# A gated mix of sliding-window attention and an MLP: the row maxima get a rate of their own by stage

## The chip, the cores and the metric

The kernel runs on one core of a Trainium2 chip. What counts is the device time of one execution, in microseconds. Engines go by the names of the profile: PE is the TensorE matmul engine (PEld its weight loads), DVE VectorE, ACT ScalarE, POOL GpSimd, SP the SyncE engine, which issues all DMAs of this kernel.

## The reference

One input `x` (2048 x 512) goes through two branches, and a sigmoid gate per row mixes them. All is float32. Cut to what is computed:

```python
# A: 32 heads of 16, window of 256 keys
qkv = x @ wqkv                              # 512 -> 1536
scores = q @ k.T * 16 ** -0.5               # each head
scores = where(0 <= i - j < 256, scores, -1e9)
a = (softmax(scores) @ v) @ wo              # heads joined, 512 -> 512

# B: an MLP with 1792 hidden columns
b = gelu(x @ w1 + b1) @ w2 + b2             # tanh form of gelu

g = sigmoid((x * gate_w).sum(-1, keepdims=True))
out = g * a + (1 - g) * b
```

## The kernel before

Every product of the dense work is done in three parts: each operand is split into a rounded high half and a low half, and `mm3` (lines 108 to 110) multiplies high by high, high by low and low by high into one PSUM tile. ACT makes the high half, DVE the low half.

The rows come in four tiles of 512. The dense work runs in this order: `qkv` for the four tiles (stage "qk"), then eight turns of the MLP (`mlp`, the table `TURNS`), each with half of the hidden columns for one tile, and at the end the output projection (`final`, stage "a"). A turn has two stages. In stage "u" seven tiles of hidden columns are made (28 calls of `mm3`), and each goes through gelu: four steps on ACT and three on DVE (lines 719 to 737). In stage "y" four blocks of 128 rows are multiplied with `w2` (again 28 calls), and DVE adds each to what is there (line 812).

The attention runs beside it, in eight groups of four heads with 16 blocks of 128 keys or queries: 128 units in all, with four products each in two passes.
- The maxima: `att_max` computes a 128 x 320 tile of scores (`sm`, line 519); DVE adds the mask and reduces it to a row's maximum (line 524, output `jm` and `M`). Every four blocks `att_rows` takes the 16 finished tiles, negates and transposes them on DVE (lines 536 to 539), and eight copies on POOL (line 546) write them into rows of `qs`, so that the second pass subtracts the maximum inside its product.
- The exponentials: `att_exp` computes the scores again, with the maxima in them (`st`, line 564), ACT takes the exponential (line 586, tile `pt`), and POOL cuts the triangles at the window's ends (line 580). After every fourth block `att_pvs` multiplies with `v` (line 608, tiles `pv_st` and `pv_sm`).

PSUM has four rings: `sm` with three buffers (the maxima, and one tile of each pv), `st` with three (the exponentials, and the other tile of the pv), `d` with two (the dense work). A maximum's product can start only when the reduction of the tile three places earlier in its ring is done.

The order of instructions on all five engines is written out by the kernel itself (`manual_schedule`). The loop at the end interleaves the two streams: for each unit `u`, and each of its four products, it calls `att_exp`, and `fill(step / 4)` draws calls of `mm3` from the generator `dense()`. In stage "u" this is done product by product, in the other stages two by two. Vector, scalar and DMA work is put off with `after(ns, ...)` in a planned time that `tick` moves on with each product. Each engine then works through its list in order, and waits only for semaphores.

Before the change the maxima have no rate of their own: in unit `u` the four maxima of unit `u + 12` (`LEAD`) are computed, one ahead of each exponentials product. The loads of the next tile of `kd` and `qd` (lines 488 and 475 to 480), `att_rows` and the first loads of `qs` (line 499) are tied to the same counter.

Of the kernel before, what the change touches and what calls it, by code (L numbers as in the profile page):

```python
# [19 lines left out]
NT = S // T  # L20
NB = T // 128
# [11 lines left out]
def gated_mix(ctx: ExitStack, tc: tile.TileContext, x, wqkv, wo, w1, b1, w2, b2, gate_w, out):  # L33
# [60 lines left out]
    for s in (0, 1):  # L94
        for k in (0, 1):
            v = own[64 * s:64 * s + 4].rearrange("r (p s) -> r s p", s=2)[:, s]
            nc.gpsimd.affine_select(out=v, in_=v, pattern=[[-2, 2]], compare_op=ALU.not_equal,
                                    fill=1.0, base=-k, channel_multiplier=1)
# [16 lines left out]
    def after(ns, fn, *args):  # L115
        now[1] += 1
        heapq.heappush(todo, (now[0] + ns, now[1], fn, args))
# [364 lines left out]
    def load_kd(g_, c):  # L482
        for t in range(max(c - 1, 0), c + 1):
            ready(t, g_, 1)
            k0 = 0 if t == c else T - W
            at = W if t == c else 0
            src = heads(SK[t], g_)[:, :, :, :, k0:].rearrange("s d u a c -> (s d u) a c")
            nc.sync.dma_start(f32(kd[0:96, slot(g_, c), :, at:at + T - k0]), src)

    def load_qd(g_, c):  # L490
        ready(c, g_, 0)
        put_pairs([f32(qd[48 * s:48 * s + 48, slot(g_, c)]) for s in range(2)], SQ[c], g_)

    def load_qs(g_, c):
        ready(c, g_, 0)
        need(("v", NT - 2, NB - 1))
        for s in range(2):
            v = f32(qs[64 * s + 4:64 * s + 52, :, c * T:(c + 1) * T])
            nc.sync.dma_start(v, part(SQ[c], g_, s).rearrange("r (a c) -> r a c", a=2))
# [405 lines left out]
    stage = ["qk"]  # L905
# [3 lines left out]
    def fill(ns):  # L909

        owed[0] += ns
        while owed[0] > 0:
            c = next(run)
            if c is None:
                owed[0] = -1e9
            else:
                owed[0] -= c
                tick(c)

    NU = NG * NKB  # L920
    NQ = NG * NT
    fill(START - AHEAD)
    for c in (0, 1):
        load_qd(0, c)
    fill(AHEAD)
    for u in range(-LEAD, NU):
        m = u + LEAD
        gm, bm = divmod(m, NKB)
        step = STEP if u >= 0 else STEP0
        for i in range(4):  # L930
            if i == 1 and m % NB == 0 and NB <= m < NU - NB:
                load_kd(*divmod(m // NB + 1, NT)), load_qd(*divmod(m // NB + 1, NT))
            if i % 2 == 0:
                pair = (i, i + 1) if stage[0] != "u" else (i,)
            elif len(pair) == 2:
                continue
            else:
                pair = (i,)
            for op, i in [(op, k) for k in pair for op in ORDER[:3]] + [("f", k) for k in pair]:
                if op == "s" and u >= 0:  # L940
                    att_exp(u // NKB, u % NKB, i)
                if op == "m" and m < NU:
                    att_max(gm, bm, i ^ XOR)
                if op == "p" and i == PVAT and u >= 1:
                    att_pvs(u - 1)
                if op == "f":
                    fill(step / 4)
        if m < NU and bm % RB == RB - 1:
            after(900, att_rows, gm, bm // RB)
        if m % NB == QAT % NB and QAT <= m < QAT + NKB:  # L950
            load_qs(0, (m - QAT) // NB)
        if u % NB == 0 and NB <= u < NU - NB:
            load_ks(*divmod(u // NB + 1, NT))
        if u % NB == 2 and NB < u < NU - 3 * NB:
            load_qs(*divmod(u // NB + 3, NT))
        if u % NB == 0 and u >= 0:
            att_load_v(*divmod(u // NB, NT))
        if u - NU + NKB in (9, 11, 13):
            load_y((u % NKB - 9) // 2)
# [11 lines left out]
RB = 4  # L971
NKB = S // 128
# [3 lines left out]
LEAD = 12  # L976
QAT = 5
# [2 lines left out]
YSWAP = 3  # L980
GELU = (700, 1500, 3600, 4600, 6000, 7000)
XAT = 3
ORDER = 'mspf'
XOR = 1
PACE = 4000.0
LAND = 7500.0
# [11 lines left out]
PVAT = 2  # L998
# [21 lines left out]
```

## Time and profile before

| what | value |
|---|---|
| median of 3 runs | 750.34 us (750.16 to 750.76) |
| profiled execution | 748.76 us, of which the span is 747.1 |
| PE busy | 732.2 us (98%), 6129 matmuls |
| PEld busy | 605.4 us (81%) |
| DVE busy | 521.9 us (70%) |
| ACT busy | 421.9 us (56%) |
| POOL busy | 372.7 us (50%) |
| granted PE clock | full, in all 40 slices but for the last us |

The profile is of one execution. A row that groups instructions gives line, engine, operation, output and inputs, shape and count; behind the first bar the busy time and the mean duration of one; behind the second the time that the engine stood idle just ahead of them, and what ended it. Rows by stretch give, for each engine, the busy time and the number of instructions, then the granted clock, the share of the DMA engines and GB/s. Matmuls are pipelined: the duration of one is its latency, the distance of two starts is what it costs, and a short wait can vanish behind the tail of the product before.

The stages of the MLP begin at 151.2 us (the first "u"), and then, in turn y, u, y and so on, at 185.5, 221.0, 254.8, 289.1, 322.2, 356.9, 391.2, 426.9, 462.8, 497.5, 531.5, 565.6, 598.9, 633.6 and 665.6; "a" begins at 698.8.

### The profile page before, as it was taken

The page shows a single profiled execution, that of the slowest core. Times are in us where ns is not written, and L with a number is a line of the kernel's source. Part 1 is how long each engine was busy: PE and PEld are TensorE (multiplying, and loading weights), DVE is VectorE, ACT ScalarE, POOL GpSimd, SP SyncE. Part 2 cuts the span into 40 slices and gives each one's busy share as a digit, 9 for nine tenths or more (in the row PEclk, how much of TensorE's full clock was granted, in tenths as well). Part 3 has the DMA queues.
Part 4 walks back from the last instruction along what each step waited for, and adds up shares of the span by engine and source line. Part 5 has one row for each costly group of instructions (what it writes and reads, how often), then busy time and mean ns, then how long its engine had stood idle before and what let it go on. Part 6 is the DMA issues. An engine that isn't in the chain of part 4 may idle for free.

```text
span 747.1 us, 17982 instructions
## 1 busy us (share of the span) xinstructions
PE 732.2 (98%) x6129; PEld 605.4 (81%) x6129; DVE 521.9 (70%) x1567; ACT 421.9 (56%) x972; POOL 372.7 (50%) x846
## 2 busy tenths in 40 slices
PE   9999999998999999999999999999999999999998
PEld 7888888876788888888887887888888888878787
DVE  4532325799768867986798689767867886784562
ACT  4434532358537844864695478447735853785541
POOL 4200000339756865786577667747765875630000
PEclk9999999999999999999999999999999999999999
DMA  9889798998895688799576989996799788538673
GB/s 324 322 275 403 256 395 279 257 321 182 257 269 139 158 235 212 183 225 268 149 174 153 228 227 227 259 244 150 180 276 234 205 227 224 136 89 263 215 268 127
DMA packets 179259, 172.12 MB, mean 230 GB/s; under 512 B 56672, under 2 KB 122976, under 8 KB 179168
## 3 DMA queue, kind: packets, MB, share of 16 engines
q1 hardware_dynamic: 179168, 170.97, 80.8%
q8 instruction: 49, 0.80, 0.5%
q14 instruction: 42, 0.34, 0.1%
HBM read 108.53 MB, written 62.39 MB: 229 GB/s over the span
## 4 chain that ended last, share of the span: by engine, by line
PE 84%; DMA 6%; DVE 3%; ACT 3%; issue 2%; SPq 1%; POOL 1%; DVEq 0%; ACTq 0%; POOLq 0%
PE sm L519 9%; PE st L564 8%; PE pv_sm L608 7%; PE y L108 6%; PE y L109 6%; PE y L110 6%; PE u L108 6%; PE u L109 5%; PE u L110 5%; PE qk L110 4%; PE qk L108 4%; PE qk L109 4%; PE v L108 2%; PE a L110 2%; PE v L110 2%
## 5 line engine op out<-in xcount | busy, mean ns | idle before, releaser
L524 DVE CUSTOM_DVE_ANT_0 jm<-sm,mask 128x320 bf16<-128x320 f32 (+4 forms) x512 | 238.5, 466 | 95.3 <-PE sm L519 58.9
L586 ACT ACTIVATE pt<-st 128x320 f32<-128x320 f32 (+4 forms) x512 | 199.7, 424 | 140.2 <-PE st L564 137.8
L580 POOL TENSOR_SCALAR_AFFINE_SELECT pt<-pt 64x256 f32<-64x256 f32 (+1 forms) x538 | 225.3, 439 | 106.7 <-ACT pt L586 96.5
L519 PE MATMUL sm<-kd,qd 96*128 96x320 f32 (+4 forms) x512 | 153.4, 311 | 6.2 <-DVE M L524 4.7
L564 PE MATMUL st<-qs,ks 128*128 128x320 f32 (+4 forms) x512 | 154.2, 309 | 1.0 <-ACT pt L586 1.0
L546 POOL CAST qs<-tt 4x256 fp32r<-4x256 f32 x256 | 127.3, 497 | 53.0 <-DVE tt L539 42.4
L519 PEld LDWEIGHTS sm<-kd,qd 96*128 96x128 f32 x512 | 96.4, 188 | 31.3 <-DVE M L524 10.7
L564 PEld LDWEIGHTS st<-qs,ks 128*128 128x128 f32 x512 | 97.3, 190 | 18.1 <-ACT pt L586 2.3
L108 PE MATMUL y<-w,h 128*128 128x512 f32 x224 | 88.5, 395 | 0.0
L109 PE MATMUL y<-w,h 128*128 128x512 f32 x224 | 88.0, 393 | 0.0
L110 PE MATMUL y<-w,h 128*128 128x512 f32 x224 | 87.9, 392 | 0.0
L108 PE MATMUL u<-mx,w 128*128 128x512 f32 x196 | 79.9, 408 | 0.0
L109 PE MATMUL u<-mx,w 128*128 128x512 f32 x196 | 77.3, 395 | 0.0
L110 PE MATMUL u<-mx,w 128*128 128x512 f32 x196 | 77.1, 393 | 0.0
L608 PE MATMUL pv_st<-pt,vbuf 64*32 64x320 f32 (+4 forms) x1408 | 73.2, 346 | 1.0 <-ACT pt L586 1.0
L608 PE MATMUL pv_sm<-pt,vbuf 64*32 64x320 f32 (+4 forms) x1408 | 73.8, 346 | 0.1
L608 PEld LDWEIGHTS pv_sm<-pt,vbuf 64*32 64x32 f32 x1408 | 50.2, 106 | 19.9 <-issue 2.3
L325 DVE TENSOR_TENSOR qke<-qk,qke 128x512 fp32r<-128x512 f32 x32 | 22.1, 689 | 46.8 <-ACT qke L322 36.8
L322 ACT ACTIVATE qke<-qk 128x512 fp32r<-128x512 f32 x32 | 19.1, 598 | 55.5 <-PE qk L110 36.5
L110 PEld LDWEIGHTS y<-w,h 128*128 128x128 f32 x224 | 42.1, 188 | 9.7
L338 POOL MEMSET vx<- 128x32 f32 x16 | 2.4, 154 | 89.6 <-DMA SQ<-qke 43.7
L608 PEld LDWEIGHTS pv_st<-pt,vbuf 64*32 64x32 f32 x1408 | 45.7, 106 | 1.1 <-ACT pt L586 1.1
(148 smaller groups left out, 1335.5 us busy)
## 6 DMA issues: line engine op xcount, KB each, us to landing
kd<-SK SPq DMA_DIRECT2D x32, 384.0 KB
qs<-SQ SPq DMA_DIRECT2D x64, 192.0 KB
mx<-XT SPq DMA_DIRECT2D x24, 512.0 KB
SQ<-qke SPq DMA_DIRECT2D x16, 512.0 KB
SK<-qke SPq DMA_DIRECT2D x16, 512.0 KB
ND<-nd SPq DMA_DIRECT2D x32, 256.0 KB
raw_w<-in_B_w_dram SPq DMA_DIRECT2D x28, 256.0 KB
ks<-SK SPq DMA_DIRECT2D x32, 192.0 KB
```

The lines of the kernel that those rows point to most:

```text
L108: nc.tensor.matmul(p, lh, rh, start=first, stop=False)
L109: nc.tensor.matmul(p, lh, rl, start=False, stop=False)
L110: nc.tensor.matmul(p, ll, rh, start=False, stop=last)
L322: nc.scalar.activation(e[:, h], p, AF.Copy)
L325: nc.vector.tensor_sub(e[:, 1 - h], p, f32(e[:, h]))
L519: nc.tensor.matmul(p[:, :w], qd[0:96, n, pr, 128 * j:128 * (j + 1)], kd[0:96, n, pr, k1 - w:k1], start=True, stop=True)
L524: nc.vector.tensor_tensor_reduce(junk[:, :w], p[:, :w], mask[:, 320 - w:320], 1.0, -3e38, ALU.add, ALU.max, M[:, 2 * (b % RB) + hb, pr:pr ...
L546: nc.gpsimd.tensor_copy(dst, src.unsqueeze(1).broadcast_to([4, 2, RB, 32]))
L564: nc.tensor.matmul(p[:, :w], ks[:, slot(g_, kb // NB), pr, at:at + 128], qs[:, pr, k0:k0 + w], start=True, stop=True)
L580: nc.gpsimd.affine_select(out=v, in_=v, pattern=[[0, v.shape[1]], [1 - 2 * e, 64]], compare_op=ALU.is_ge, fill=0.0, base=-e, channel_multi ...
L586: nc.scalar.activation(pt[:, hf, pr, :w], p[:, :w], AF.Exp, scale=SCALE)
L608: nc.tensor.matmul(pv[r // 64][32 * i:32 * i + 32, q - c * T:e - c * T], vts[g_, b // NB][r:r + 64, v:v + 32], rhs(r), start=start, stop=s ...
```

## The change

The maxima get a counter (`made`) and an account (`credit`). Ahead of each exponentials product `maxima` adds to the account what the table `MAXIMA` has for the current stage: 1 in "qk" and "a", 0.86 in "u", 1.16 in "y". As long as the account holds a whole one, `next_max` emits the next maximum, with the loads and row work that hang on its number. The account holds two at most. `LEADS` bounds how far ahead of the exponentials the maxima may be: at least 10 units, at most 12, where it was always 12. `att_rows` is now set 1400 ns of planned time behind the last maximum of its group (900 behind the end of the unit before), the first loads of `qs` 600 ns behind. The other loads keep their place in the loop over units.

```diff
+    made, credit = [0], [0.0]
+
+    def next_max():
+
+        m, i = divmod(made[0], 4)
+        made[0] += 1
+        gm, bm = divmod(m, NKB)
+        if i == 1 and m % NB == 0 and NB <= m < NU - NB:
+            load_kd(*divmod(m // NB + 1, NT)), load_qd(*divmod(m // NB + 1, NT))
+        att_max(gm, bm, i ^ XOR)
+        if i == 3 and bm % RB == RB - 1:
+            after(1400, att_rows, gm, bm // RB)
+        if i == 3 and m % NB == QAT % NB and QAT <= m < QAT + NKB:
+            after(600, load_qs, 0, (m - QAT) // NB)
+
+    def maxima(at):
+
+        credit[0] = min(credit[0] + (MAXIMA[stage[0]] if at >= 0 else 1), 2)
+        low, high = at + 4 * LEADS[0], min(at + 4 * LEADS[1] + 1, 4 * NU)
+        while made[0] < high and (credit[0] >= 1 or made[0] < low):
+            credit[0] -= 1
+            next_max()
+
     for u in range(-LEAD, NU):
-        m = u + LEAD
-        gm, bm = divmod(m, NKB)
         step = STEP if u >= 0 else STEP0
         for i in range(4):
-            if i == 1 and m % NB == 0 and NB <= m < NU - NB:
-                load_kd(*divmod(m // NB + 1, NT)), load_qd(*divmod(m // NB + 1, NT))
             if i % 2 == 0:
                 pair = (i, i + 1) if stage[0] != "u" else (i,)
...
-            for op, i in [(op, k) for k in pair for op in ORDER[:3]] + [("f", k) for k in pair]:
-                if op == "s" and u >= 0:
-                    att_exp(u // NKB, u % NKB, i)
-                if op == "m" and m < NU:
-                    att_max(gm, bm, i ^ XOR)
-                if op == "p" and i == PVAT and u >= 1:
+            for k in pair:
+                maxima(4 * u + k)
+                if u >= 0:
+                    att_exp(u // NKB, u % NKB, k)
+                if k == PVAT and u >= 1:
                     att_pvs(u - 1)
-                if op == "f":
-                    fill(step / 4)
-        if m < NU and bm % RB == RB - 1:
-            after(900, att_rows, gm, bm // RB)
-        if m % NB == QAT % NB and QAT <= m < QAT + NKB:
-            load_qs(0, (m - QAT) // NB)
+            for k in pair:
+                fill(step / 4)
...
-ORDER = 'mspf'
+MAXIMA = {"qk": 1.0, "u": 0.86, "y": 1.16, "a": 1.0}
+LEADS = (10, 12)
```

In the list of instructions the change looks as follows. In the stage "u" that begins at 426.9 us, on PE, between two calls of `mm3` for the tile `u_8` and the pv that follows; `sm` is a maximum's product, `st` an exponentials product. Before:

```order
L110 MATMUL u_8_6186<-mx_4405,w_8_5241 128x512
L519 MATMUL sm_12_0_6235<-kd,qd 128x320
L564 MATMUL st_0_1_6239<-qs,ks 128x320
L519 MATMUL sm_12_3_6242<-kd,qd 128x320
L564 MATMUL st_0_2_6246<-qs,ks 128x320
L608 MATMUL pv_3_sm<-pt_10_5826,vbuf 32x64
```

And after:

```order
L110 MATMUL u_8_6186<-mx_4386,w_8_5238 128x512
L564 MATMUL st_0_1_6231<-qs,ks 128x320
L519 MATMUL sm_12_0_6238<-kd,qd 128x320
L564 MATMUL st_0_2_6242<-qs,ks 128x320
L608 MATMUL pv_3_sm<-pt_10_5818,vbuf 32x64
```

One exponentials product has no maximum ahead of it, and the maxima are one further behind from here on. In the stages "u" from the second to the seventh this happens four times each, in the first three times: 29, 28, 28, 29, 29 and 28 maxima stand in them where 33, 32, 32, 33, 33 and 32 stood.

In the stage "y" that begins at 391.2 us, on PE, early in the first block of rows (`y_00`). Before:

```order
L519 MATMUL sm_3_1_5597<-kd,qd 128x320
L564 MATMUL st_7_0_5601<-qs,ks 128x320
L519 MATMUL sm_3_0_5604<-kd,qd 128x320
L564 MATMUL st_7_1_5609<-qs,ks 128x320
L108 MATMUL y_00_5556<-w_3_1884,h_3_5285 128x512
```

And after:

```order
L519 MATMUL sm_2_1_5581<-kd,qd 128x320
L564 MATMUL st_7_0_5585<-qs,ks 128x320
L519 MATMUL sm_2_0_5588<-kd,qd 128x320
L519 MATMUL sm_2_3_5592<-kd,qd 128x320
L564 MATMUL st_7_1_5596<-qs,ks 128x320
L108 MATMUL y_00_5540<-w_3_1884,h_3_5277 128x512
```

Two maxima stand one behind the other, and the burst holds three. This happens three times in the first stage "y" and four times in each of the next six, 27 times in all. (In this place the maxima are four products, one block, further back than before.)

On DVE, in the stage "u" that begins at 426.9 us, from the gelu step of tile `h_9` to the transpose of a group's rows. `w` is the low half of a weight tile, `jm` and `M` are a reduction and the reading of its result. Before:

```order
L737 TENSOR_TENSOR h_9_6393<-x1h_9_6393_6399,h_9_6393 128x512
L524 ISA jm_0_1_6523,M_0_6520<-sm_0_1_6521,mask 128x64
L524 ISA M_0_6520 128x1
L182 TENSOR_TENSOR w_11_6511<-raw_w_6383,w_11_6511 128x512
L536 TENSOR_SCALAR nm<-M_12_6213 128x8x2
L537 SCALAR_TENSOR_TENSOR nm<-M_12_6213,nm 128x8x2
L539 STREAM_TRANSPOSE tt<-nm 128x256
```

And after:

```order
L737 TENSOR_TENSOR h_9_6389<-x1h_9_6389_6395,h_9_6389 128x512
L182 TENSOR_TENSOR w_11_6505<-raw_w_6379,w_11_6505 128x512
L524 ISA jm_15_3_6528,M_12_6213<-sm_15_3_6526,mask 128x320
L524 ISA M_12_6213 128x1
L731 SCALAR_TENSOR_TENSOR x1h_10_6460_6466<-sqh_10_6460_6467,x1h_10_6460_6466 128x512
L524 ISA jm_15_2_6544,M_12_6213<-sm_15_2_6542,mask 128x320
L524 ISA M_12_6213 128x1
L725 SCALAR_TENSOR_TENSOR sqh_11_6532_6539<-sqh_11_6532_6539,x1h_11_6532_6538 128x512
L536 TENSOR_SCALAR nm<-M_12_6213 128x8x2
L537 SCALAR_TENSOR_TENSOR nm<-M_12_6213,nm 128x8x2
L539 STREAM_TRANSPOSE tt<-nm 128x256
```

The row work of a group now stands behind two more gelu steps, since its last maxima come later.

## The prediction

> **What bounds the kernel now.** I read the page first, then the span cut into the stages of the dense work, then the waits in front of the maxima's products, then single rows.
>
> ```profile
> PE 732.2 (98%) x6129; PEld 605.4 (81%) x6129; DVE 521.9 (70%) x1567; ACT 421.9 (56%) x972; POOL 372.7 (50%) x846
> L524 DVE CUSTOM_DVE_ANT_0 jm<-sm,mask 128x320 bf16<-128x320 f32 (+4 forms) x512 | 238.5, 466 | 95.3 <-PE sm L519 58.9
> L519 PE MATMUL sm<-kd,qd 96*128 96x320 f32 (+4 forms) x512 | 153.4, 311 | 6.2 <-DVE M L524 4.7
> ```
>
> TensorE is busy for 732.2 of 747.1 us, so nearly all of the span is its own work, and 14.9 us of visible idle time are left. The change gives TensorE neither more nor fewer products, so it can only win idle time back, or add some. The second and third rows say where DVE can cause it: a maximum's product (`sm`, L519) needs one of three PSUM buffers, and a buffer comes free when DVE has reduced it (L524, the largest single consumer of DVE).
>
> The stages, one row each: first products (u) begin at 151.20, 254.80 is a second-product stage (y), and so on in turn.
>
> ```profile
> core 0: us, PE busy (x) PEld busy (x) DVE busy (x) ACT busy (x) POOL busy (x), PEclk, DMA share, GB/s
> 151.20:185.50 34.30, 31.44 (x209) 24.31 (x208) 31.71 (x94) 25.07 (x52) 21.80 (x38) 1.00 0.92 240
> 185.50:221.00 35.50, 34.53 (x345) 28.72 (x344) 24.69 (x86) 17.05 (x42) 24.40 (x62) 1.00 0.92 266
> 221.00:254.80 33.80, 33.74 (x320) 28.67 (x319) 28.51 (x92) 25.27 (x58) 23.87 (x51) 1.00 0.59 141
> 254.80:289.10 34.30, 34.30 (x345) 28.73 (x344) 23.84 (x84) 16.16 (x40) 23.24 (x60) 1.00 0.88 235
> 289.10:322.20 33.10, 33.10 (x318) 27.84 (x317) 29.62 (x93) 25.56 (x58) 22.69 (x47) 1.00 0.76 187
> 356.90:391.20 34.30, 33.64 (x318) 27.90 (x317) 30.25 (x92) 27.17 (x62) 22.92 (x48) 1.00 0.67 161
> 391.20:426.90 35.70, 34.51 (x342) 28.46 (x341) 27.27 (x91) 18.28 (x44) 25.40 (x61) 1.00 0.76 183
> 426.90:462.80 35.90, 34.50 (x320) 28.09 (x319) 32.53 (x99) 28.02 (x64) 24.87 (x48) 1.00 0.93 226
> 462.80:497.50 34.70, 34.38 (x343) 28.58 (x343) 25.30 (x87) 16.98 (x42) 23.37 (x60) 1.00 1.04 260
> 497.50:531.50 34.00, 33.80 (x320) 28.23 (x319) 26.62 (x89) 25.51 (x57) 22.82 (x50) 1.00 0.61 150
> ```
>
> DVE carries 28.5 to 32.5 us in a u stage (the three gelu steps per tile come on top of the maxima) and 24 to 27 in a y stage. The u stage at 289.10 is the limit case: DVE 29.62 of 33.10 us (89%) and no idle time on TensorE. Where DVE has more (151.20: 92%, 426.90: 91%, both with weight splits on it) TensorE idles 2.86 and 1.40 us, and the y stage behind inherits the queue (0.97, 1.19, 0.32). So TensorE is held up by DVE in three pairs of stages, while DVE has 7 to 10 us to spare in each y stage. This is one such wait:
>
> ```profile
> 465.73 0.31 PE L519 MATMUL sm<-kd,qd 96*128 96x320 f32 x1
> 465.88 0.31 PE L564 MATMUL st<-qs,ks 128*128 128x320 f32 x1
> 466.51 0.42 PE L519 MATMUL sm<-kd,qd 96*128 96x320 f32 x1 [0.32 <-DVE M L524]
> ```
>
> Start to start, a 320-wide product takes 0.15 us; here the next maximum starts 0.63 after the `st`, so 0.48 us are lost while the row shows 0.32 as idle. The idle figures above are therefore lower bounds of what is lost.
>
> **The change, part by part.**
>
> 1. Four maxima fewer in each of the u stages two to seven, three fewer in the first (counted in the new order); as many more in the y stage behind each. The total is unchanged. What is one worth to DVE?
>
> ```profile
> 446.49 0.49 DVE L524 CUSTOM_DVE_ANT_0 jm<-sm,mask 128x320 bf16<-128x320 f32 x1
> 446.90 0.09 DVE L524 DVE_READ_ACCUMULATOR2_ANT M<- 128x1 f32 x1
> 447.13 0.49 DVE L524 CUSTOM_DVE_ANT_0 jm<-sm,mask 128x320 bf16<-128x320 f32 x1
> 447.55 0.08 DVE L524 DVE_READ_ACCUMULATOR2_ANT M<- 128x1 f32 x1
> 447.55 0.69 DVE L737 TENSOR_TENSOR h<-x1h,h 128x512 fp32r<-128x512 f32 x1
> 448.15 0.48 DVE L524 CUSTOM_DVE_ANT_0 jm<-sm,mask 128x320 bf16<-128x320 f32 x1
> ```
>
> A maximum followed by a maximum holds DVE for 0.64 us (446.49 to 447.13), one followed by a gelu step for 0.42 (447.13 to 447.55). I take 0.5, since both neighbours are common in a u stage. A u stage thus hands DVE back 3 x 0.5 = 1.5 us (the first; 1.3 to 1.9) or 4 x 0.5 = 2.0 us (1.7 to 2.6).
>
> While DVE is what TensorE waits for, each microsecond taken off DVE is one off the wait, up to the time that is lost there. By pairs of stages:
> - 151.20 with 185.50: relief 1.5, idle 2.86 + 0.97, more than the relief. Gain 1.5.
> - 356.90 with 391.20: relief 2.0. Idle 0.66 + 1.19 = 1.85; by length, against the undisturbed 33.10 and 34.30, 1.2 + 1.4 = 2.6. Gain 1.9.
> - 426.90 with 462.80: relief 2.0, idle 1.40 + 0.32 = 1.72, by length 2.8 + 0.4 = 3.2. Here part of the relief finds another wait:
>
> ```profile
> 445.89 0.70 DVE w L182
> 446.60 0.33 SPq L170
> ...
> 448.63 6.54 DMA rb<-RD
> 455.26 0.32 DVE num L662
> ...
> 458.20 0.35 PE sm L519
> ```
>
>  DVE frees a raw-weight buffer, SP goes on to the reciprocals' load, that lands after 6.54 us, and DVE's multiplication stands in its queue for it; 9 us pass whatever DVE has to do meanwhile. I take 1.4 of 2.0.
> - The rest: 497.50 idles 0.20, 221.00 0.06; I take 0.3.
>
> Together 5.1 us (4.2 at 0.42 a maximum, 7.7 at 0.64 and without the load's wait).
>
> 2. In the y stages, 27 calls make two maxima without an exponentials' product between, so that up to three meet three buffers. Bounds: nothing, as in the y stage at 254.80, whose bursts of two cost 0.00 idle; or 0.48 each, the wait quoted above, 27 x 0.48 = 13.0 us. It is nearer to the first: the stage with the most DVE work would have 27.27 + 4 x 0.64 = 29.8 us of some 34.3 (87%), below the 89% that idled nowhere, but in bursts. I take 0.04 each, 1.1 us, for the bursts behind a pv, which holds one of the same three buffers, and for those at a y stage's start, where gelu steps are still queued.
>
> 3. The maxima lag by up to four, about one block of the attention. `att_rows` and the eight copies on POOL come that much later, plus 500 ns of planned time. 33 pairs of products in 34.3 us are 1.04 us a pair, 4.2 us a block; before, a group of rows was complete seven blocks (29 us) ahead of its first use. Six remain. Cost nothing; the cover is those six blocks.
>
> 4. The loads of `kd` and `qd` move behind those of `ks` and `vbuf` in SP's queue, with the maxima they belong to.
>
> ```profile
> 151.12 6.87 DMA qd<-SQ
> 277.03 2.65 SPq L488 DMA_DIRECT2D kd<-SK  x2
> 296.18 0.30 SPq L488 DMA_DIRECT2D kd<-SK  x1
> ```
>
>  One tile of 16 maxima is loaded while the one before is used up; tiles follow at 16 to 19 us here. At 1.16 a pair, 16 maxima take 13.8 pairs, 14.4 us; SP needs about 5 us for the five issues and the landing 6.87. Some 2.5 us remain, so I cost it at nothing; without that cover, a stall of a few tenths per y stage.
>
> Sum: -5.1 + 1.1 = -4.0 us. The profiled execution took 748.76 us (span 747.1, 1.7 around it), which makes 744.8. Its time lies 1.6 under the median of 750.34; on the median the same gain gives 746.3, which is the forecast.
>
> The page "SBUF — State Buffer" of the Trainium skill (Who interferes with whom) says that a DVE instruction with two SBUF inputs contends with a GpSimd instruction that reads SBUF, through an exclusive lock, while one with a single SBUF input does not. By that rule gelu steps would suffer and maxima would not, and a u stage with fewer maxima would hold its gelu steps closer together under POOL's selections. The rows for it:
>
> ```profile
> L725 DVE SCALAR_TENSOR_TENSOR sqh<-sqh,x1h 128x512 f32<-128x512 f32 x56 | 43.1, 769 | 2.7 <-ACT sqh L722 2.2
> L737 DVE TENSOR_TENSOR h<-x1h,h 128x512 fp32r<-128x512 f32 x56 | 42.4, 757 | 0.9 <-ACT h L734 0.6
> L812 DVE SCALAR_TENSOR_TENSOR yo<-y,ya 128x512 f32<-128x512 f32 x32 | 21.9, 685 | 1.2 <-DMA ya<-YA 0.6 <-PE y L110 0.5
> ```
>
> Steps of equal size take 757 to 769 ns on average with both inputs in SBUF, and 685 with one in PSUM: about 0.08 us each, 1.7 for 21 steps of a u stage. These steps are as many after the change, and POOL as busy, so the sum does not move.
>
> **Rivals.**
> - The waits are not all the queue's (chance 0.20). DVE and ACT pass each gelu tile to and fro, and a wait of DVE for ACT is not shortened by fewer maxima. For it: the groups above show waits for ACT, 2.2 and 0.6 us. Against it: these are small beside 6.2 us in front of `sm`. If only a third of 5.1 is won, 1.7 us, and no burst waits: 748.6.
> - The bursts decide (0.22), the case on the other side. If a second maximum in a call finds its buffer unreduced, TensorE stops in stages that now run free. At 5.1 / 27 = 0.19 us per burst the gain is gone; at 0.30 the sum is +3.0, 753.3. For it: the wait shown at 466.51 is just such a second maximum of a burst. Against: it stands at the end of a u stage's queue, which gets shorter.
> - The relief is eaten (0.08): gelu steps stretch by a further 0.1 us when they stand closer, 21 x 0.1 = 2.1 us a stage, as much as is taken off. Then 750.3. Against: the means above, at POOL busy 22.7 to 24.9 of 33 us throughout. The mechanism is the port rule cited.
> - That the change does not do what it says is excluded by the order: 28 or 29 maxima stand in u stages where 32 or 33 stood.
>
> **How the numbers follow.** Forecast 0.50, with a range of its own of 742.6 (7.7 gained, bursts free) to 748.0 (4.2 gained, bursts at 0.07). A difference of 0.2%, 1.5 us, is about what a measurement of this kernel can tell from none. Faster: 0.50 + 0.20 = 0.70; same 0.08; slower 0.22. The range of 742.6 to 752.5 holds the forecast, the first and third rivals and the milder bursts; it leaves out the costlier bursts.
>
> **What would show it.** In the changed profile, stages behind 151, 357 and 427 us should be shorter by 1 to 2 us each, with DVE down about 2 us in u stages and up as much in y stages; the idle time before `sm` (6.2 us) should fall to 2 or 3. Waits of `sm` on DVE in the middle of y stages would show the bursts; waits of `st` on POOL, or of `sm` on a `kd` transfer, would show that points 3 or 4 were wrong. An unchanged idle time in the u stages with less DVE work would show the first rival.

## The result and the profile after

The changed kernel takes 758.11 us (median of six runs, 754.75 to 759.59) where the kernel before takes 750.55 beside it (750.16 to 753.05). The ratio is 1.0088, with a 95% interval of 1.0067 to 1.0109: slower by 0.9%, where 0.5% faster was forecast, and outside the range of 742.6 to 752.5. The profiled execution took 759.59 us, with a span of 757.9.

The page of the changed kernel, for the engines and for the products of the attention:

```profile
PE 736.2 (97%) x6129; PEld 610.1 (81%) x6129; DVE 524.0 (69%) x1567; ACT 422.0 (56%) x972; POOL 366.5 (48%) x846
L519 PE MATMUL sm<-kd,qd 96*128 96x320 f32 (+4 forms) x512 | 149.2, 311 | 8.8 <-DVE M L524 4.7
L608 PE MATMUL pv_sm<-pt,vbuf 64*32 64x320 f32 (+4 forms) x1408 | 75.4, 347 | 1.4 <-POOL pt L580 0.9
L608 PE MATMUL pv_st<-pt,vbuf 64*32 64x320 f32 (+4 forms) x1408 | 74.4, 347 | 1.9 <-POOL pt L580 1.2
```

The idle time ahead of the maxima's products was to fall from 6.2 to 2 or 3 us; it rose to 8.8. The pv (L608) now waits for POOL's selections, which the kernel before shows in no row of its page. The signs that the prediction had named for its points 3 and 4, waits of `st` on POOL and of `sm` on `kd`, do not appear. The stages, cut as before, begin at 151.40 (u), 186.10 (y), 359.10 (u), 393.50 (y), 429.60 (u), 467.60 (y) and 536.60 (y):

```profile
core 0: us, PE busy (x) PEld busy (x) DVE busy (x) ACT busy (x) POOL busy (x), PEclk, DMA share, GB/s
151.40:186.10 34.70, 31.16 (x206) 24.42 (x205) 31.00 (x88) 24.81 (x52) 19.35 (x34) 1.00 0.93 241
186.10:221.80 35.70, 34.82 (x347) 29.07 (x347) 24.78 (x90) 17.25 (x42) 25.45 (x65) 1.00 0.95 258
359.10:393.50 34.40, 33.03 (x315) 27.26 (x314) 29.67 (x86) 26.89 (x62) 21.60 (x46) 1.00 0.62 162
393.50:429.60 36.10, 34.98 (x346) 28.83 (x346) 28.90 (x97) 18.27 (x44) 25.67 (x63) 1.00 0.72 191
429.60:467.60 38.00, 34.81 (x315) 28.60 (x314) 30.77 (x90) 27.70 (x63) 23.22 (x45) 0.96 0.83 212
467.60:503.80 36.20, 35.52 (x348) 29.21 (x347) 27.48 (x97) 17.34 (x43) 24.63 (x63) 1.00 0.96 256
536.60:576.80 40.20, 37.23 (x348) 30.97 (x347) 27.10 (x95) 16.57 (x41) 24.83 (x63) 0.96 0.81 215
```

Four maxima that move take 4 x 0.15 = 0.6 us from a u stage to the y stage behind it, so pairs are to be compared. The first pair takes 70.4 us (69.8 before), the one at 359 70.5 (70.0), the one at 429 74.2 (70.6). In none is anything won, though DVE did get less to do in the u stages: by 0.7 us in the first, 0.6 in the one at 359 and 1.8 in the one at 429. The largest loss is in the y stage at 536.60, with 40.2 us; its counterpart before is one of 34.1. Here is its stall, first on DVE, then on PE:

```profile
564.88 0.85 DVE L662 TENSOR_TENSOR num<-num,rb 128x512 f32<-128x512 f32 x1 [2.69 <-DMA rb<-RD]
566.52 0.35 DVE L650 RECIPROCAL den<-den 128x32 f32<-128x32 f32 x1 [0.78 <-DMA den<-ND]
...
567.28 0.42 PE L519 MATMUL sm<-kd,qd 96*128 96x320 f32 x1 [1.84 <-DVE M L524]
567.97 0.61 PE L519 MATMUL sm<-kd,qd 96*128 96x320 f32 x1 [0.27 <-DVE nd L632]
...
568.64 0.63 PE L108 MATMUL y<-w,h 128*128 128x512 f32 x1
569.07 0.63 PE L109 MATMUL y<-w,h 128*128 128x512 f32 x1
```

PE's row names the maximum (L524), but DVE was in time with that until it stood in its queue for two loads of the softmax division: the reciprocals (`rb`, 2.69 us) and the next denominators (`den`, 0.78). The stage at 429.6 has the same, with 1.86 us of idle time at 443.95. SP's rows show why these loads are late. In the changed kernel:

```profile
546.76 0.55 SPq L505 DMA_DIRECT2D vbuf<-SV  x1
547.35 1.14 SPq L488 DMA_DIRECT2D kd<-SK  x2
...
550.11 1.30 SPq L653 DMA_DIRECT2D RD<-den  x1
...
555.56 0.60 SPq L658 DMA_DIRECT2D rb<-RD  x1
```

And in the kernel before, at the same place of the program:

```profile
532.71 1.42 SPq L488 DMA_DIRECT2D kd<-SK  x2
...
540.04 0.55 SPq L505 DMA_DIRECT2D vbuf<-SV  x1
540.69 0.60 SPq L653 DMA_DIRECT2D RD<-den  x1
...
544.11 0.60 SPq L658 DMA_DIRECT2D rb<-RD  x1
```

`vbuf` has to wait until the pv has read the old values. Before, `kd` and `qd` had gone ahead of it, and the division's store (`RD`) came 0.65 us behind it; now five loads for the maxima stand in between, and the store comes 3.35 us behind.

### The profile page after: what moved, and what is told of

It reads as the page before. It is cut to its first block, busy times and chain, and to the rows that moved or that the text cites. A ratio compares the mean times of both kernels' runs of the same rounds, so it can differ in the third digit from the quotient of the medians.

```text
span 757.9 us, 17953 instructions
## 1 busy us (share of the span) xinstructions
PE 736.2 (97%) x6129; PEld 610.1 (81%) x6129; DVE 524.0 (69%) x1567; ACT 422.0 (56%) x972; POOL 366.5 (48%) x846
## 4 chain that ended last, share of the span: by engine, by line
PE 76%; DMA 8%; DVE 4%; ACT 3%; POOL 3%; issue 3%; SPq 2%; DVEq 0%; ACTq 0%; POOLq 0%
PE sm L519 8%; PE st L564 7%; PE pv_sm L608 6%; PE u L108 5%; PE y L108 5%; PE y L109 5%; PE y L110 5%; PE u L109 5%; PE u L110 5%; PE qk L110 4%; PE qk L108 4%; PE qk L109 4%; DMA den<-ND 3%; POOL pt L580 2%; PE a L110 2%
## 5 line engine op out<-in xcount | busy, mean ns | idle before, releaser
L524 DVE CUSTOM_DVE_ANT_0 jm<-sm,mask 128x320 bf16<-128x320 f32 (+4 forms) x512 | 238.4, 466 | 92.9 <-PE sm L519 53.5
L580 POOL TENSOR_SCALAR_AFFINE_SELECT pt<-pt 64x256 f32<-64x256 f32 (+1 forms) x538 | 223.4, 435 | 107.8 <-ACT pt L586 96.7
L519 PE MATMUL sm<-kd,qd 96*128 96x320 f32 (+4 forms) x512 | 149.2, 311 | 8.8 <-DVE M L524 4.7
L546 POOL CAST qs<-tt 4x256 fp32r<-4x256 f32 x256 | 122.6, 479 | 67.7 <-DVE tt L539 56.8
L109 PE MATMUL u<-mx,w 128*128 128x512 f32 x196 | 77.9, 397 | 0.0
L608 PE MATMUL pv_sm<-pt,vbuf 64*32 64x320 f32 (+4 forms) x1408 | 75.4, 347 | 1.4 <-POOL pt L580 0.9
L608 PE MATMUL pv_st<-pt,vbuf 64*32 64x320 f32 (+4 forms) x1408 | 74.4, 347 | 1.9 <-POOL pt L580 1.2
L608 PEld LDWEIGHTS pv_sm<-pt,vbuf 64*32 64x32 f32 x1408 | 52.6, 106 | 20.5 <-issue 2.4
L608 PEld LDWEIGHTS pv_st<-pt,vbuf 64*32 64x32 f32 x1408 | 47.4, 106 | 2.5 <-POOL pt L580 1.6
L725 DVE SCALAR_TENSOR_TENSOR sqh<-sqh,x1h 128x512 f32<-128x512 f32 x56 | 42.8, 764 | 5.2 <-ACT sqh L722 4.8
```

The source lines that it names most:

```text
L109: nc.tensor.matmul(p, lh, rl, start=False, stop=False)
L519: nc.tensor.matmul(p[:, :w], qd[0:96, n, pr, 128 * j:128 * (j + 1)], kd[0:96, n, pr, k1 - w:k1], start=True, stop=True)
L524: nc.vector.tensor_tensor_reduce(junk[:, :w], p[:, :w], mask[:, 320 - w:320], 1.0, -3e38, ALU.add, ALU.max, M[:, 2 * (b % RB) + hb, pr:pr ...
L546: nc.gpsimd.tensor_copy(dst, src.unsqueeze(1).broadcast_to([4, 2, RB, 32]))
L580: nc.gpsimd.affine_select(out=v, in_=v, pattern=[[0, v.shape[1]], [1 - 2 * e, 64]], compare_op=ALU.is_ge, fill=0.0, base=-e, channel_multi ...
L608: nc.tensor.matmul(pv[r // 64][32 * i:32 * i + 32, q - c * T:e - c * T], vts[g_, b // NB][r:r + 64, v:v + 32], rhs(r), start=start, stop=s ...
```

## The experiments

Beside each stands the ratio to the kernel before, measured on the same chip, with its 95% interval. The expectations give the theories letters. Those that mattered in the end are A, the order of SP's queue delays the division; C, the shift itself costs, since it puts maxima where DVE still has gelu steps; and D, the lag of the maxima costs by what hangs on it, in its sharper form P: it moves POOL's copies to a bad place in POOL's order.

### The order of SP's queue

**`e1_ks_behind_kd`**: the changed kernel, with the loads of `ks` and `vbuf` held until `kd` and `qd` are issued.

```diff
+            while held:
+                held.pop(0)()            # behind load_kd, load_qd in next_max
...
-            load_ks(*divmod(u // NB + 1, NT))
+            held.append(lambda n=u // NB + 1: load_ks(*divmod(n, NT)))
...
-            att_load_v(*divmod(u // NB, NT))
+            held.append(lambda n=u // NB: att_load_v(*divmod(n, NT)))
```

> The changed kernel with one thing undone: the loads of ks and vbuf of a tile wait until kd and qd of that tile have been issued, so that SP's queue has nearly the order of the kernel before; the maxima keep their rates of 0.86 and 1.16. Theory A (SP's queue: kd and qd, now behind the vbuf load that waits for a pv, push the division's transfers back by 4 to 6 us, and DVE stands on them): the waits of DVE on den and rb at 439, 443, 565 and 566 us (6.8 us in all) go, and the time comes down to 746 to 751. Theory B (bursts of maxima in the y stages, three on three buffers): the bursts are all still there, so 755 to 758.

Measured: 757.80, ratio 1.0087 (1.0057 to 1.0118). Nothing is won. The stall in the y stage shown above is gone (36.1 us), but DVE stands for a division's load elsewhere:

```profile
338.84 0.78 DVE L662 TENSOR_TENSOR num<-num,rb 128x512 f32<-128x512 f32 x1 [3.02 <-DMA rb<-RD]
```

**`e2_kd_behind_ks`**: the reverse, in the kernel before: only `kd` and `qd` go behind `ks` and `vbuf`.

```diff
-            if i == 1 and m % NB == 0 and NB <= m < NU - NB:
-                load_kd(*divmod(m // NB + 1, NT)), load_qd(*divmod(m // NB + 1, NT))
...
             att_load_v(*divmod(u // NB, NT))
+        if m % NB == 0 and NB <= m < NU - NB:
+            load_kd(*divmod(m // NB + 1, NT)), load_qd(*divmod(m // NB + 1, NT))
```

> The kernel before with one thing added: the five loads of kd and qd stand behind the loads of ks and vbuf of the same unit; the maxima keep one rate of 1. Theory A: the division's transfers come later by the time of five issues, 2.7 us or more, and somewhere DVE stands on them: 753 to 758. Theory B: no burst is added, so 750 to 751.

Measured: 757.75, ratio 1.0083 (1.0055 to 1.0111). The order of five loads alone costs as much as the whole change, and nearly all of it at one place:

```profile
446.45 0.35 DVE L650 RECIPROCAL den<-den 128x32 f32<-128x32 f32 x1 [5.17 <-DMA den<-ND]
...
447.41 0.64 PE L519 MATMUL sm<-kd,qd 96*128 96x320 f32 x1 [5.03 <-DVE nd L632]
```

DVE stood 5.17 us at a reciprocal of 0.35 us, and TensorE 5.03 behind it. So theory A is shown as a cost of its own. By the first run it is not the only one.

**`e3_rate_one`**: the changed kernel with all rates 1; what is left is the new loop and its delays of 1400 and 600 ns.

```diff
-MAXIMA = {"qk": 1.0, "u": 0.86, "y": 1.16, "a": 1.0}
+MAXIMA = {"qk": 1.0, "u": 1.0, "y": 1.0, "a": 1.0}
```

> The changed kernel with all four rates set to 1: the account alone, the row work set at 1400 instead of 900 ns and the first qs loads at 600. The order on SP differs from before in a few places only. Theories A and B both expect the time of before, 749.5 to 751.5; more would mean that the row work's or the first loads' place costs something by itself.

Measured: 750.92, ratio 0.9993 (0.9972 to 1.0015). The account by itself costs nothing that can be measured here.

### The division

**`e4_division_late`**: the changed kernel, with the steps of the division planned later.

```diff
-DIVS = ((5000, 7500, 13500, 20000, 22000), (4500, 5700, 8500, 17000, 18500))
+DIVS = ((8000, 10500, 16500, 27000, 29000), (4500, 5700, 8500, 17000, 18500))
```

> The changed kernel with the three DVE steps of the division planned later (reciprocal at 8000 instead of 5000 ns, multiplication at 27000 instead of 20000, transfers between them by the same 3000). SP's queue keeps kd and qd behind ks and vbuf. Theory A: DVE comes to the steps when the transfers have landed, the 6.8 us of waits mostly go, 748 to 753. Theory B: no change, 755 to 758.

Measured: 756.25, ratio 1.0062 (1.0039 to 1.0085). **`e5_order_and_division`**, the edits of `e1` and `e4` together:

> Both repairs together: ks and vbuf behind kd and qd as in the first experiment, and the division's DVE steps planned later as in the fourth. DVE should no longer stand on the division's transfers anywhere in the MLP. If those waits were all the loss, 748 to 751. If shifting the maxima by stage itself costs time (bursts, or exponentials and selections that come late), the time stays at 754 to 757.

Measured: 757.68, ratio 1.0077 (1.0059 to 1.0095). **`e8_before_division_late`**, the later division in the kernel before:

> The kernel before, with the division's DVE steps planned later and nothing else. It has few waits of DVE on the division's transfers (0.5 us in the MLP stages), so 748.5 to 751; a higher time would mean that the later division costs something by itself, which would then stand in the fourth and fifth kernels too.

Measured: 750.70, ratio 0.9987 (0.9972 to 1.0003). The later division is free by itself, and in the changed kernel it takes the waits of DVE for `den` and `rb` out of the MLP, but for 0.4 us (in `e5` none is left). Yet with order and division mended about six microseconds are still lost. The waits now stand at the start of the stages y, ahead of the pv, and where the exponentials wait for ACT. The shift must cost something else.

### When the shift takes place

**`e6_rate_lags_8`**: `e5`, but the rate follows the stage eight exponentials products later, since gelu steps of the last tiles of u run on into y.

```diff
+        lagged.append(stage[0])
-        credit[0] = min(credit[0] + (MAXIMA[stage[0]] if at >= 0 else 1), 2)
+        credit[0] = min(credit[0] + (MAXIMA[lagged[-1 - LAG]] if at >= 0 else 1), 2)
...
+LAG = 8
```

> The fifth kernel with the rates lagging the stage by 8 exponentials products (about 8 us), because the gelu steps of a u stage reach DVE some 8 us after its products, into the y stage. Theory C (the waits at a y stage's start, at 401 us and 472 us in the changed kernel, stay because the y rate begins while DVE is still in gelu): 2 to 4 us faster than the fifth kernel, and the waits at those places go. If the place of the rate does not matter: equal to the fifth.

Measured: 754.14, ratio 1.0042 (1.0027 to 1.0056), 3.5 us under `e5`, as theory C expects, though it brings back only part of the loss.

**`e7_no_bursts`**: `e5`, but never more than one maximum ahead of an exponentials product; an extra one goes between the two calls of `mm3`.

```diff
-        while made[0] < high and (credit[0] >= 1 or made[0] < low):
+        n = 0
+        while made[0] < high and (credit[0] >= 1 or made[0] < low) and n < 1:
...
+                if k == pair[0] and len(pair) == 2:
+                    rest(4 * u + k)
```

> The fifth kernel with the same rates, but never more than one maximum ahead of an exponentials product: a second one that is owed stands between the two dense calls of the pair. Theory B (bursts): 3 to 5 us faster than the fifth kernel. If bursts cost nothing: equal to it.

Measured: 767.88, ratio 1.0205 (1.0171 to 1.0238), ten microseconds above `e5`. The waits of the maxima for DVE are 3.8 us in sum, where `e5` has 4.9; the new idle time is ahead of the pv, for POOL.

```profile
L608 PE MATMUL pv_st<-pt,vbuf 64*32 64x320 f32 (+4 forms) x1408 | 78.6, 358 | 8.7 <-POOL pt L580 7.2
```

That led to the lag: with one maximum at most the account catches up later, and the maxima stay behind for longer.

### The lag, and where POOL's copies stand

**`e9_lag_alone`**: `e5` with all rates 1 and a constant lag of one unit.

```diff
-MAXIMA = {"qk": 1.0, "u": 0.86, "y": 1.16, "a": 1.0}
-LEADS = (10, 12)
+MAXIMA = {"qk": 1.0, "u": 1.0, "y": 1.0, "a": 1.0}
+LEADS = (10, 11)
```

> The kernel with order and division mended (757.68), all rates 1, and the maxima at most 11 units ahead of the exponentials instead of 12: the lag is there everywhere and constant, the shift between stages is gone. Theory D (the lag itself costs: rows and the copies on POOL come later, and stand in POOL's order ahead of the selections that pv waits for): 754 to 757, and waits of pv on POOL (L580) and the first stage u at about 36 us as in the mended kernel. Theory C (it is the shift of the maxima between stages that costs): 750.5 to 751.5, and those waits as in the kernel before.

Measured: 767.93, ratio 1.0243 (1.0227 to 1.0260). Without any shift the lag costs 17 us.

**`e10_ahead_of_before`** and **`e11_ahead_rate_lags`** were to take the lag away instead, with the maxima 13 units ahead (`LEAD = 13`, `LEADS = (11, 13)`, `START` 2750 ns earlier), in `e5` and in `e6`.

> The kernel with order and division mended (757.68), its rates 0.86 and 1.16 kept, but the maxima 13 units ahead at the start of a stage u and 11 at least, so that they are never later than before, up to rounding (the loop starts one unit earlier, by 2.75 us of planned time). Theory D (the lag costs): about 751. Theory C (the shift costs): 757 to 758, as with the smaller lead, with the waits of the maxima's products for DVE at the start of stages y (some 1 us each at about 394 and 470 us) unchanged.

> As the run with the maxima 13 units ahead, and the rate follows the stage only 8 exponentials products later, when the gelu steps of the last tiles of u are off DVE. Theory D and C both count: 750 or a little below if lag and late gelu steps were all; 754 (as with the lagging rate alone) if the lag does not matter; under 748 only if the relief of the stages u, estimated at 4 to 5 us, at last comes through.

Measured: 857.42 (ratio 1.1409, 1.1375 to 1.1442) and 844.18 (1.1240, 1.1214 to 1.1266). Both say nothing of the theories. With the lead of 13, the loads of `ks` that `e1`'s edit holds go out up to three blocks late, and the exponentials wait for them, 77.9 us in the first of the two:

```profile
L564 PE MATMUL st<-qs,ks 128*128 128x320 f32 (+4 forms) x512 | 158.7, 319 | 80.6 <-DMA ks<-SK 77.9
```

**`e12_before_rows_late`**: the kernel before, with the row work of a group put off by one block, on DVE and POOL. No product and no load moves.

```diff
-            after(900, att_rows, gm, bm // RB)
+            after(5100, att_rows, gm, bm // RB)
```

> The kernel before; only the row work of a group (negation, transpose, the eight copies on POOL) is put off by one block, 4.2 us of planned time. No product and no load moves. Theory P (the phase: the copies then stand in POOL's order ahead of the selections that the next pv needs, and DVE's row work beside the pv's eviction): about as slow as the run with the constant lag, 760 to 768, with waits of pv on POOL (L580) of 5 us or more in sum. Theory L (the maxima's own lag costs, not the rows'): 750 to 752.

Measured: 765.85, ratio 1.0202 (1.0178 to 1.0226): 16 us, though the rows are still there six blocks ahead of their first use. The page shows where (`pv_st` waits for POOL another 2.8):

```profile
L608 PE MATMUL pv_sm<-pt,vbuf 64*32 64x320 f32 (+4 forms) x1408 | 79.1, 353 | 4.6 <-POOL pt L580 4.3
```

POOL's order shows how these waits arise. The kernel before, ahead of a pv that begins at 537.52 and waits for nothing (L546 are the copies, L580 the selections):

```profile
520.73 3.49 POOL L546 CAST qs<-tt 4x256 fp32r<-4x256 f32 x6
...
527.71 0.83 POOL L546 CAST qs<-tt 4x256 fp32r<-4x256 f32 x2
...
531.90 5.44 POOL L580 TENSOR_SCALAR_AFFINE_SELECT pt<-pt 64x256 f32<-64x256 f32 x12 [1.00 <-ACT pt L586]
```

And the run with the rows one block later, at the same pv:

```profile
537.89 2.07 POOL L546 CAST qs<-tt 4x256 fp32r<-4x256 f32 x4
...
542.50 2.07 POOL L546 CAST qs<-tt 4x256 fp32r<-4x256 f32 x4
544.63 5.66 POOL L580 TENSOR_SCALAR_AFFINE_SELECT pt<-pt 64x256 f32<-64x256 f32 x12
...
550.10 0.25 PE L608 MATMUL pv_sm<-pt,vbuf 64*32 64x64 f32 x2 [0.74 <-POOL pt L580]
```

The pv comes every four blocks, and so does a group's row work. Before, the copies begin about 17 us ahead of the pv, right behind the one before, and when the last selections are due POOL waits for ACT (1.00). One block later they begin 9.9 us ahead (537.89 to 547.76, where the pv begins), in the midst of the selections that this pv needs; POOL has no gap left, and TensorE waits for its last selections.

These waits, 7.1 us, are not all of the 16. The waits of the maxima for DVE rise as well, from 4.7 to 8.5 us, and the rest lies in TensorE's busy time, 740.8 us for 732.2, in which short waits vanish and in which the clock was halved twice. The negation and the transpose on DVE move together with the copies, and no run moves the copies alone. So the 16 us are shown for the place of the row work, and for the copies' place on POOL the 7.1.

The changed kernel drifts in and out of this place as its lag goes from none to a block. Its pv that wait for POOL for more than 0.1 us are three (at 180, 267 and 543 us); six or all of their eight copies begin 9.7 to 10.4 us ahead. Counted from a group's first copy, the copies begin 8 to 14 us ahead of all of the first 29 pv in `e9` and in `e12`, of 13 in `e7`, 9 in `e6`, 3 in the changed kernel and 1 in `e5`, and of none in the kernel before. The third of the three:

```profile
533.17 3.12 POOL L546 CAST qs<-tt 4x256 fp32r<-4x256 f32 x5
...
538.81 0.93 POOL L546 CAST qs<-tt 4x256 fp32r<-4x256 f32 x1
539.81 4.67 POOL L580 TENSOR_SCALAR_AFFINE_SELECT pt<-pt 64x256 f32<-64x256 f32 x12
...
543.71 0.30 PE L608 MATMUL pv_st<-pt,vbuf 64*32 64x64 f32 x4 [0.57 <-POOL pt L580]
```

**`e13_lag_rows_in_phase`**: `e9`, with the row work back at its old place in the loop, that is, later by three more blocks.

```diff
-            after(1400, att_rows, gm, bm // RB)
+            whole.append((gm, bm // RB))
...
+        if u % RB == RB - 1:
+            while whole:
+                after(900, att_rows, *whole.pop(0))
```

> The run with the constant lag of one unit (767.93); only the row work is tied to the place in the loop at which the kernel before has it, so that it comes three blocks later still, four behind the kernel before, a whole period. Theory P: 750 to 753, and pv waits for POOL no more than before (1 to 2 us). If lateness of the rows as such cost: above 768.

Measured: 753.11, ratio 1.0037 (1.0024 to 1.0050). Fourteen to fifteen of the 17 us are gone although the rows come still later, so it is the place of the row work and not its lateness. (By the count above, the copies are at the bad place ahead of none of the first 29 pv.) The lateness, four blocks now, costs about 3 us, and the waits for it, 3.9 us in sum, stand where the first groups are due:

```profile
172.08 0.58 PE L564 MATMUL st<-qs,ks 128*128 128x320 f32 x1 [3.00 <-POOL qs L546]
```

**`e14_shift_rows_in_phase`** and **`e15_lagging_rate_in_phase`**: the same edit in `e5` and in `e6` (`M` gets a third buffer; `g1` takes the place of `z` to make room).

> The kernel with order and division mended and the rates 0.86 and 1.16 (757.68), its row work tied to the old place in the loop (a third buffer for M is needed). Theory P alone: the waits of pv on POOL go, 749 to 752. If the shift between stages costs by itself as well (the late gelu steps): 753 to 755.

> As the last, and the rate follows the stage only 8 exponentials products later (754.14 without the rows in phase). If phase and late gelu steps were all that ate the relief: 745 to 748, below the kernel before. If the relief of the stages u does not exist: 750 to 752.

Measured: 755.03 (1.0061, 1.0040 to 1.0081) and 759.96 (1.0134, 1.0110 to 1.0158). The first is within the uncertainty of `e5` and at the upper end of what was expected; the second is worse than `e6` and missed it. Where a lag of a few products pushes a whole group into the next period, the exponentials wait for its copies, 6.0 us in the first run and 8.5 in the second:

```profile
L564 PE MATMUL st<-qs,ks 128*128 128x320 f32 (+4 forms) x512 | 154.5, 311 | 10.7 <-POOL qs L546 8.5
```

### The shift alone

**`e16_shift_alone`**: the changed kernel, with the rows at their old place and the maxima 12 to 13 units ahead, so that no group is ever late and POOL's order is that of the kernel before; the later division of `e4`.

```diff
-            after(1400, att_rows, gm, bm // RB)
+            whole.append((gm, bm // RB))
...
-        credit[0] = min(credit[0] + (MAXIMA[stage[0]] if at >= 0 else 1), 2)
-        low, high = at + 4 * LEADS[0], min(at + 4 * LEADS[1] + 1, 4 * NU)
+        credit[0] = min(credit[0] + (MAXIMA[stage[0]] if at >= 0 else 13 / 12), 2)
+        low, high = min(at + 4 * LEADS[0] + 1, 4 * NU), min(at + 4 * LEADS[1] + 1, 4 * NU)
...
-LEADS = (10, 12)
+LEADS = (12, 13)
```

> The changed kernel with its rates 0.86 and 1.16, but the maxima are 12 to 13 units ahead (the thirteenth is made up in the stage qk, at 13 maxima per 12 products), the row work hangs at the old place in the loop, so that POOL's order is word for word that of the kernel before, and the late division steps of the earlier runs. What is left of the change is the shift of the maxima between the stages. If the relief of the stages u is real and phase, lateness and queue were all that ate it: 746 to 749. If the gelu steps that run on into stage y cost as much as the relief: 750 to 752. If the shift itself costs: 753 or more.

Measured: 754.99, ratio 1.0058 (1.0042 to 1.0074). The waits of the pv on POOL are gone but for 0.5 us, and the shift by itself still costs 4.6. The start of a stage y shows it (465.4 us), here on PE and then on DVE:

```profile
470.33 0.41 PE L519 MATMUL sm<-kd,qd 96*128 96x320 f32 x1 [0.76 <-DVE M L524]
...
468.01 0.68 DVE L731 SCALAR_TENSOR_TENSOR x1h<-sqh,x1h 128x512 f32<-128x512 f32 x1
...
469.02 0.85 DVE L725 SCALAR_TENSOR_TENSOR sqh<-sqh,x1h 128x512 f32<-128x512 f32 x1
...
470.84 0.80 DVE L737 TENSOR_TENSOR h<-x1h,h 128x512 fp32r<-128x512 f32 x1
```

Five microseconds into y, DVE still has gelu steps of u to do, and the extra maxima meet them. Here the largest loss of `e16` lies. The u stage ahead of this y takes 34.9 us, where it took 35.9 before, and the y stage 38.6, where it took 34.7:

```profile
430.50:465.40 34.90, 34.06 (x316) 27.30 (x315) 30.04 (x89) 27.55 (x62) 23.81 (x48) 1.00 0.92 228
465.40:504.00 38.60, 37.36 (x348) 30.43 (x348) 28.31 (x99) 17.94 (x44) 23.17 (x61) 0.96 0.90 254
```

The visible idle time in this y stage is 1.1 us. From 472.10 to 475.50, behind these waits, the granted clock is 0.50, and that is part of the loss as well.

**`e17_shift_lags`**: `e16` with the edit of `e6`.

> As the last, and the rate follows the stage only 8 exponentials products later. If the late gelu steps are what is left of the cost: 2 to 4 us under the last run, 743 to 748. If they are not: the same time within 1 us.

Measured: 751.01, ratio 1.0016 (1.0001 to 1.0032): 4.0 us under `e16` beside it, as expected, though not down to the 743 to 748 that were expected with it. Of the loss 0.7 us are left, at the edge of what can be measured; nothing is won over the kernel before. The lagging rate also moves less: of the up to four maxima that leave a u stage in `e16`, two or three leave it here, since a u stage begins at the rate of y. Its stages at 358.1 (u), 391.9 (y), 426.6 (u) and 462.6 (y):

```profile
358.10:391.90 33.80, 33.12 (x317) 27.65 (x316) 29.97 (x90) 26.95 (x62) 24.00 (x47) 1.00 0.69 167
391.90:426.60 34.70, 34.70 (x343) 28.88 (x343) 28.05 (x93) 18.39 (x44) 25.28 (x61) 1.00 0.75 190
426.60:462.60 36.00, 34.46 (x317) 27.57 (x316) 31.52 (x95) 27.16 (x62) 24.30 (x49) 1.00 0.84 211
462.60:498.20 35.60, 35.33 (x347) 29.57 (x346) 27.02 (x92) 17.94 (x44) 22.39 (x60) 1.00 1.00 271
```

The first pair takes 68.5 us, where it took 70.0 before; the second 71.6, where it took 70.6. The pair at 151.9 takes 70.4, where it took 69.8. In the y stage at 531.8 TensorE stands still for 1.61 us (at 543.66) for which the profile names no releaser; this cause is open.

## Why the prediction was wrong

- **Point 1, the relief (5.1 us)**, did not come. The step that failed is "while DVE is what TensorE waits for, each microsecond taken off DVE is one off the wait", and it failed in two ways. First, not all of the idle time that was counted was DVE's to give back: in the kernel before, the 0.66 us at 356.90 are a wait of a pv for ACT, 0.7 of the 2.86 at 151.20 are waits of `st` for ACT, and 1.24 of the 1.40 at 426.90 are the reciprocals' load, which the prediction had seen. Even in `e16`, with the full shift and POOL's order as before, the u stages idle for 3.2 us (at 152.3), 0.86 (at 360.5) and 0.84 (at 430.5), where it was 2.86, 0.66 and 1.40; only the third fell. Second, the step took DVE's work of a stage to be done in that stage. But gelu steps lag the products that feed them, so that part of the work of u is done in y, and taking maxima out of u and into the start of y moves them towards DVE's load. In `e17`, which moves them later and fewer of them, the pair at 358 wins 1.5 us of the 1.9 forecast for it, most of it in y (whose 1.19 us of idle time are gone); the pair at 427 loses 1.0 where 1.4 was to be won, and the pair at 152 loses 0.6 where 1.5 was to be won. How much the full relief would be worth without its cost in y no run shows.
- **The first rival**, waits that are not the queue's, was nearer in part. Of the 1.5 us that `e17` idles in the u stage at 426.6, 0.8 are waits of `st` for ACT. And DVE's waits for ACT ahead of the three gelu steps rose from 4.0 us in the kernel before to 8.1 in the changed one (9.0 in `e17`), so that part of the time taken off DVE became idle time of DVE. Most of that lies in stages in which TensorE had no idle time; in the u stages at 151, 359 and 430 the rise is 0.2, 0.2 and 1.0. The row of one of the three steps after the change (before, it had waited 2.2 us for ACT):

```profile
L725 DVE SCALAR_TENSOR_TENSOR sqh<-sqh,x1h 128x512 f32<-128x512 f32 x56 | 42.8, 764 | 5.2 <-ACT sqh L722 4.8
```

- **Point 2, the bursts (1.1 us)**, had the place ("those at a y stage's start, where gelu steps are still queued") and not the size. What the lagging rate saves, 4.0 us from `e16` to `e17`, is what the extra maxima cost there, with the stretch at half clock that follows their waits in `e16`; whether it is the bursts or only the number of the maxima stays open. `e17`'s y stage at 391.9 has the extra maxima further on, and no idle time. The second rival, on the slower side, thus had a real mechanism, with 4.0 for its 8.1 (27 x 0.30). (The wait at 466.51 that the prediction took for a second maximum of a burst has an `st` ahead of it, so it does not show one.) `e7` can't tell what a burst costs in itself, since spreading them changed the lag as well.
- **Point 3, "cost nothing; the cover is those six blocks"**, failed, and not for want of cover. Lateness was asked about, and four blocks of it cost about 3 us (`e13`). Not asked was which instructions the copies then stand ahead of in POOL's order. The row work one block later is 16 us by itself (`e12`). In the changed kernel, which lags so only at times, the pv's waits for POOL come to 2.1 us.
- **Point 4, "I cost it at nothing"**, failed in the same way. The loads that move were in time themselves: no maximum waits for `kd`. What stands behind them in SP's queue was not priced: the division's store, hence its loads, hence DVE, hence every maximum. It is worth six microseconds in the kernel before (`e2`). In the profile of the changed kernel its two stalls, 1.86 us at 443.95 and 1.84 + 0.27 at 567.28, and the slow products behind them make an estimated 6 of the span's 10.8.
- **The third rival**, relief eaten by gelu steps that grow by 0.1 us, is not what happened. The three steps take 764 (L725), 739 (L731) and 775 ns (L737) on average in the changed kernel, where they took 769, 744 and 757: 8 ns more per tile of hidden columns, where the rival needs 300.

These costs don't add up to the loss. If they did, order and division mended would have won 6 us, and they won nothing (`e5`): a repair shifts the time of all that follows, and another wait appears. What each costs where it stands alone is shown by `e2` for SP's order, by `e12`, and by `e9` against `e13`, for the place of the row work, and by `e16` against `e17` for the extra maxima at the start of y; how the 7.6 us of the changed kernel divide among them stays open.

## What to carry to other kernels

When an instruction moves in a queue that works strictly in order, it isn't enough to ask whether it is still in time: ask what stands behind it at the new place, on each queue, and follow that to its end. Work that recurs with the same period as its consumer has a phase, and a small lag changes the phase by as much as it changes the lateness. Before load is moved from a stage with a busy engine to the next, cut the engine's time by the work's origin, since its queue lags the stage that feeds it.

## What had not been expected of the hardware

A stall of TensorE can cost more than its length. After the stop of 1.84 us at 567.28 the changed kernel's dense products start 0.43 us apart (568.64, 569.07) instead of 0.23, with a granted clock of 0.50:

```profile
568.40:571.00 2.60, 2.60 (x8) 2.14 (x8) 1.58 (x5) 0.44 (x1) 0.00 (x0) 0.50 0.97 239
```

Six dense products at 0.2 us more each make 1.2 us on top of the 1.84. A longer stop does not always do so: in `e14`, after 2.62 us, they start 0.24 apart.

```profile
447.48 0.41 PE L564 MATMUL st<-qs,ks 128*128 128x320 f32 x1 [2.62 <-POOL qs L546]
...
448.02 0.40 PE L108 MATMUL u<-mx,w 128*128 128x512 f32 x1
448.26 0.39 PE L109 MATMUL u<-mx,w 128*128 128x512 f32 x1
```

The half rate lasts 3.41 us behind each of the changed kernel's two stalls (444.92 to 448.33 and 567.80 to 571.21), and two such stretches behind the 5.03 us of `e2` (446.59 to 453.42). In the 3.41 us ahead of these stretches, TensorE is visibly idle for 1.86 and 1.95 us in the changed kernel, and all the time in `e2`.

The Trainium skill, page "TensorE: Matmul & The Clock Gate" (Part 1: The HAM clock gate), says that the clock is halved after at least one idle window of about 3.4 us, and that this window runs freely. The stretches of 3.41 us agree with such a window. That it takes a whole idle window does not agree: less than 2 us of visible idle time in one were enough. That one stop is followed by the half rate and another isn't would suit a window that runs freely, since a stop can fall across its border. What decides it is not shown here: in `e16` the half rate follows 3.41 us with only 1.1 us of visible idle time (468.69 to 472.10).
